# First forward stage of a fast Fourier transform on sums and differences of mirrored rows, as 24x24 matrices on 32x32 tiles

## The chip, the cores and the metric

The kernel runs on one core of a Trainium2 chip. The metric is the device time of one execution in microseconds (us). The engines named below are TensorE (PE in the profile, its weight loads PEld), VectorE (DVE), ScalarE (ACT), GpSimd (POOL) and SyncE (SP), whose queue issues most of the transfers. One slice of the work, a "slot", is explained below.

## The reference

A filter in the frequency domain over the sequence of each batch, then two dense layers with a GELU between them:

```python
batch, seq, dim = (8, 3008, 256)
X = np.fft.rfft(x, axis=1)
F = (filt_r + 1j * filt_i)[None, :, :]
y = np.fft.irfft(X * F, n=x.shape[1], axis=1)
...
h = x @ w_in                      # 24064 x 256 times 256 x 2048
g = 0.5 * h * (1.0 + erf(h * inv_sqrt2))
return (g @ w_out).astype(np.float32)
```

The input of the dense layers is the filtered sequence. Inputs and output are float32.

## The kernel before

The length 3008 is 47 x 64, and the transform is done in two factors each way. Row n of a batch is written as n = 64 m + w, with m from 0 to 46 and w from 0 to 63. Stage 1 (`s1`) is a transform over m, a multiplication with a table of 47 rows and 48 columns (24 frequencies, real and imaginary). Stage 2 (`s2`) is a transform over w with twiddles in the table, and is multiplied with the filter. Stages 3 and 4 (`s3`, `s4`) go back. Between stages 1 and 2, and between 3 and 4, the data pass through a buffer in DRAM (R1 and R2), which exchanges the axes: stores by SP, then loads (`r1`, `r2`). Stage 4 writes the bf16 ring `y_sb`, from which the dense layers read.

The dense layers go by tiles of 512 rows. A slot is one `mm1` (two matmuls of 512 columns for one of 16 blocks of hidden units, then GELU on ScalarE) and a quarter of the `mm2` of the tile before (four matmuls of 256 columns); every eight slots VectorE copies a result `ost` out of PSUM, and SP stores it. The slots of the first tile, 0 to 15, have no `mm2`. Batch 0 is transformed ahead of all slots by special routines (`c1` to `c4`). The stages of batches 1 to 7 are put between the slots by a list written by hand: `put(slot, function, batch, part)` files a step, and ahead of each slot its steps are issued. Each engine has one queue and works it off in that order, so a step on VectorE stands behind all VectorE steps filed before it.

Stage 1 of a batch is four calls `s1(b, c)`, at `s1 + int(c * n1)`: for batch 1 from slot 0 in steps of 4, for the others from `hi - 94` in steps of 3.5, where `hi` is the first slot that reads the batch. `r1` follows at slot 15 or `hi - 80`, the second stage at slot 25 or `hi - 69`. A call takes 16 of the 64 values of w:

- x lies in SBUF with m on partitions 0 to 46 for w below 32, and on 64 to 110 for the rest. `load_x` (L83) brings it from GpSimd's queue, which also turns float32 into bf16; eight loads per batch. In the second stage of the batch before, `load_next` files them one by one behind a `gate`, a copy of one element that makes GpSimd wait for the second stage's product.
- Eight matmuls (L300) of 47x64 by 512 columns run on four 64x64 tiles of TensorE into four PSUM banks, three of tag `f` (three in all) and one of tag `h` (three, else used by `mm1`).
- VectorE empties the four banks into `a_sb` (L275), and SP stores it to R1 in four transfers (L309) of 48 partitions.

The table `T1s` for this is made by `table_1_tiles` on GpSimd from the table of batch 0. GpSimd's queue at the start is: loads of x for batch 0, loads of the filters in three groups, `w_in`, copies of the filter to the other half of the partitions (`dup_filters`, L97), `T1s`, x of batch 1, `w_out`.

Of the kernel before, what the change touches and what calls it, by code (L numbers as in the profile page):

```python
# [9 lines left out]
AF = mybir.ActivationFunctionType  # L10
ALU = mybir.AluOpType
FP32 = mybir.dt.float32
BF16 = mybir.dt.bfloat16
I32 = mybir.dt.int32
PI = math.pi


NA, NB = 47, 64
K1 = 24
HB = 32  # L20
RND = 12582912.0
# [8 lines left out]
class _Mix:  # L30
    def __init__(self, ctx, tc, x, filt_r, filt_i, w_in, w_out, out):
        self.tc, self.nc = tc, tc.nc
        self.x, self.filt_r, self.filt_i = x, filt_r, filt_i
        self.w_in, self.w_out, self.out = w_in, w_out, out
        self.B, self.S, self.D = x.shape
        self.DFF = w_in.shape[1]
        assert self.S == NA * NB and self.D == 256 and self.DFF == 2048
        pool = lambda name, bufs, **kw: ctx.enter_context(tc.tile_pool(name=name, bufs=bufs, **kw))
        P = bass.MemoryType.PSUM
        self.const = pool("const", 1)  # L40
        self.px = pool("px", 2)
        self.pa = pool("pa", 3)
        self.pb = pool("pb", 4)
        self.pp = pool("pp", 4)
        self.pv = pool("pv", 3)
        self.pd = pool("pd", 4)
        self.pool = pool
        self.po = pool("po", 3)
        self.py = pool("py", 1)
        self.pg = pool("pg", 2)  # L50
        self.small = pool("small", 1)
        self.dram = pool("dram", 2, space=bass.MemoryType.DRAM)
        c = self.const
        self.T1 = c.tile([2 * NA, 96], BF16, name="T1")
        self.T2 = c.tile([128, K1, 2, NB], BF16, name="T2")
        self.T3 = c.tile([128, K1, 2, NB], BF16, name="T3")
        self.T4 = c.tile([96, NA, 2], BF16, name="T4")
        self.T4c = c.tile([96, NA, 2], BF16, name="T4c")
        self.F = c.tile([128, 2, K1, 256], BF16, name="F")
        self.w_in_sb = c.tile([128, 2, self.DFF], BF16, name="w_in_sb")  # L60
        self.w_out_sb = c.tile([128, 16, self.D], BF16, name="w_out_sb")
        self.ps, self.st = {}, {}
        self.flip = 0
# [11 lines left out]
    def load_x(self, b, lo=0, n=32, hs=(0, 1)):  # L75
        nc = self.nc
        if lo == 0 and 0 in hs:
            self.st[b, "x"] = self.px.tile([128 if b else 2 * NA, HB, 256], BF16, tag="x", name="x_sb")
        xt, o = self.st[b, "x"], 64 if b else NA
        xv = self.x[b].rearrange("(n1 h w) d -> h n1 w d", h=2, w=HB)  # L80
        for w in range(lo, lo + n, 8):
            for h in hs:
                nc.gpsimd.dma_start(out=xt[h * o:h * o + NA, w:w + 8, :], in_=xv[h][:, w:w + 8, :])  # L83

    def load_filters(self, k0, k):

# [14 lines left out]
        g = self.po.tile([1, 1], BF16, tag="gate", name="gate")  # L101
        self.nc.gpsimd.tensor_copy(out=g, in_=t)  # L102

    def load_next(self, b, p, c, h):

        self.gate(self.st[b, "p", p][0:1, 0:1])
        self.load_x(b + 1, 8 * c, 8, (h,))

    def load_w_in(self):
        wi = self.w_in.rearrange("(dc p) j -> p dc j", p=128)  # L110
# [14 lines left out]
    def table_1(self, g):  # L125

        nc, ts = self.nc, self.nc.vector.tensor_scalar
        col = lambda name: g.tile([128, 1], FP32, name=name)
        off = g.tile([128, 2, K1], FP32, name="off")
        nc.vector.memset(off[:, 0, :], 0.25)  # L130
        nc.vector.memset(off[:, 1, :], 0.5)
        h, n1, hs, hc = col("h"), col("n1"), col("hs"), col("hc")
# [144 lines left out]
            self.nc.vector.tensor_scalar(out=out, in0=in_, scalar1=scale, scalar2=None, op0=ALU.mult)  # L277


    def table_1_tiles(self, g):  # L280

        v = self.nc.gpsimd
        self.T1s = g.tile([128, 64], BF16, name="T1s")
        v.memset(self.T1s, 0.0)
        for r in (0, 64):
            v.tensor_copy(out=self.T1s[r:r + NA, 0:48], in_=self.T1[0:NA, 0:48])

    def s1(self, b, c):

        nc = self.nc  # L290
        if c == 0:
            self.st[b, "R1"] = self.dram.tile([NB, 48, 256], BF16, tag="R1", name="R1")
        a = self.pa.tile([128, 2, 4, 256], BF16, tag="a", name="a_sb")
        x = self.st[b, "x"]
        ps = [[self.bank("ps_s1", "h" if i == h == 0 else "f") for h in range(2)] for i in range(2)]
        for i in range(2):
            for r in range(2):
                for h in range(2):
                    w = 8 * c + 4 * r + 2 * i
                    nc.tensor.matmul(ps[i][h][64 * r:64 * r + 64, :], lhsT=self.T1s[64 * h:64 * h + NA],  # L300
                                     rhs=x[64 * h:64 * h + NA, w:w + 2, :], start=True, stop=True)
        for i in range(2):
            for h in range(2):
                self._evac(a[:, h, 2 * i:2 * i + 2, :].rearrange("p a b -> p (a b)"), ps[i][h], False)
        o = self.st[b, "R1"].rearrange("n q c -> q n c")
        for r in range(2):
            for h in range(2):
                w = HB * h + 8 * c + 4 * r
                nc.sync.dma_start(out=o[:, w:w + 4, :], in_=a[64 * r:64 * r + 48, h])  # L309

    def r1(self, b, c):
        bt = self.pb.tile([128, 6, 256], BF16, tag="b", name="b_sb")
# [219 lines left out]
def kernel(  # L532
# [40 lines left out]
    m.vt = m.pg.tile([128, 2, 97, 32], BF16, tag="g", name="vt_sb")  # L573
    for k, n in ((0, 4), (4, 8), (12, 12)):
        m.load_filters(k, n)
    m.load_w_in()

    nc.gpsimd.memset(m.vt[:, :, 96, :], 0.0)
# [35 lines left out]
    for q in range(1, 7):  # L614
        if q < 6:
            m.c2(2 * q)
            if q + 2 < 6:
                m.c1t(q + 2, (act,))
            if q != 3:
                m.warm_up(2)  # L620
            m.c2(2 * q + 1)
        if q < 6:
            m.c3(2 * q - 2)
            if q == 3:
                m.table_3(2)
                m.table_3_copy(2, True)
            else:
                m.warm_up(1)
        else:
            m.c3(10, 1)  # L630
            m.warm_up(1)
            m.c3(11, 1)
    m.warm_up(2)
    m.T1p = g.tile([2 * NA, 2, K1, 2], BF16, name="T1p")
    nc.gpsimd.tensor_copy(out=m.T1p, in_=m.T1.rearrange("p (h r k) -> p h k r", h=2, r=2))
    m.table_1_tiles(g)
    m.load_x(1)
    m.load_w_out(0)
    m.load_w_out(8)
    m.weights_4(g)  # L640
# [14 lines left out]
    def put(slot, f, *a):  # L655
        at.setdefault(slot, []).append((f, a))
# [4 lines left out]
    for b in range(1, B):  # L661
        hi = first(b)
        if b == 1:
            s1, n1, r1, s2, n2, r2, s4, n4 = 0, 4, 15, 25, 2.8, 61, 68, 0.72
        else:
            s1, n1, r1, s2, n2, r2, s4, n4 = hi - 94, 3.5, hi - 80, hi - 69, 3.5, hi - 24, hi - 17, 1
        for u in range(16):
            put(s4 + int(u * n4), m.s4, b, u // 2, u % 2)
        for c in range(4):
            put(s1 + int(c * n1), m.s1, b, c)  # L670
            put(r1, m.r1, b, c)
            put(r2, m.r2, b, c)
        for p in range(12):
            put(s2 + int(n2 * p), m.s2, b, p)
            put(s2 + int(n2 * p) + 4, m.s3, b, p)
        if b + 1 < B:
            for i in range(8):
                put(s2 + int(n2 * (i + 2)), m.load_next, b, i + 2, i // 2, i % 2)

    put(20, m.table_4, m.T4, m.T1p, m.wt, "f", "act")  # L680
    for s in range((NT + 1) * 16):
# [38 lines left out]
```

## Time and profile before

| what | us |
|---|---|
| time, median of 3 runs | 772.94 (771.6 to 773.65) |
| profiled execution: its span | 771.8 |
| TensorE busy | 763.0 (99%) |
| VectorE busy | 399.0 (52%) |
| ScalarE busy | 567.8 (74%) |
| GpSimd busy | 63.7 (8%) |
| matmuls of stage 1 (L300), 224, mean of one | 0.389 |
| evictions of stage 1 (L275 into `a_sb`), 112, mean of one | 0.683 |
| loads of x on GpSimd (L83), 64, mean of one | 0.516 |
| stores to R1 (L309), 112, median from issue to landing | 2.1 |
| loads from R1 (L315), 28, median from issue to landing | 4.2 |

In a busy column, rows that overlap on a pipelined engine count their own length; the ends of matmuls are modelled, so start-to-start distances say more than the mean of one. A timeline line gives start, length, engine, line of the code, operation, tiles (out<-in), shape, how many were merged, and in brackets how long the engine was idle before and for whom. A group line ends with busy us, the mean of one in ns, and the idle time before it. In a line by windows there follow, for each engine in the order PE, PEld, DVE, ACT, POOL, the busy us and in brackets the count, then the granted clock (1.00 is full), the busy share of the transfer engines and GB/s.

### The profile page before, as it was taken

What the parts mean: (1) busy time and instruction counts of PE and PEld (TensorE: products, weight loads), DVE (VectorE), ACT (ScalarE), POOL (GpSimd) and SP (SyncE); (2) the same over time, 40 slices, a digit from 0 to 9 for tenths busy, and PEclk for the clock granted to TensorE, in tenths of its full rate; (3) what the DMA queues carried; (4) which work ended last, traced back from release to release, by engine and by line L of the source; (5) the groups of instructions that cost most, each with busy time, mean ns of one, the idle gap of its engine ahead of it and who ended that gap; (6) DMA issues with size and microseconds to landing.
All of it is one profiled execution on the core that took longest, in us unless ns stands there. A gap on an engine that the chain in (4) does not pass through costs nothing.

```text
span 771.8 us, 15047 instructions
## 1 busy us (share of the span) xinstructions
PE 763.0 (99%) x6057; PEld 527.2 (68%) x6057; DVE 399.0 (52%) x735; ACT 567.8 (74%) x978; POOL 63.7 (8%) x157
## 2 busy tenths in 40 slices
PE   8999999999999999999999999999999999999998
PEld 4757675676776766667677767666776776766666
DVE  8966755464545645457463664637646366411011
ACT  7879855897568975699656996579865798666663
POOL 8701100010000200011000110001100000000000
PEclk9999999999999999999999999999999999999999
DMA  9795645466153661636516465355553422410111
GB/s 151 130 191 130 146 113 125 130 128 150 54 147 102 136 162 41 191 77 124 142 54 181 85 133 123 81 152 97 122 137 82 138 83 69 123 42 28 42 42 55
DMA packets 87270, 85.66 MB, mean 111 GB/s; under 512 B 6688, under 2 KB 77472, under 8 KB 87200
## 3 DMA queue, kind: packets, MB, share of 16 engines
q1 hardware_dynamic: 78816, 68.70, 31.6%
q0 software_dynamic: 8384, 16.00, 14.7%
q8 instruction: 47, 0.77, 0.4%
q14 instruction: 23, 0.19, 0.1%
HBM read 54.00 MB, written 46.66 MB: 130 GB/s over the span
## 4 chain that ended last, share of the span: by engine, by line
PE 97%; DMA 1%; DVE 1%; POOL 0%; issue 0%; SPq 0%; DVEq 0%; POOLq 0%
PE ps_o L513 42%; PE ps_h L486 42%; PE ps_s L373 2%; PE ps_s L348 2%; PE ps_s L323 2%; PE ps_s L300 2%; DMA x_sb<-in_x_dram 1%; PE ps_c L434 1%; PE ps_c3t L449 0%; PE ps_c L412 0%; DMA d_sb<-R 0%; PE ps_warm L267 0%; POOL x_sb L83 0%; PE ps_c L463 0%; DVE T3i L260 0%; PE ps_c1t L399 0%
## 5 line engine op out<-in xcount | busy, mean ns | idle before, releaser
L489 ACT ACTIVATE g_sb<-ps_h 128x512 bf16<-128x512 f32 x752 | 437.9, 597 | 182.7 <-PE ps_h L486 172.0
L513 PE MATMUL ps_o<-w_out_sb,g_sb 128*128 128x256 bf16 x2992 | 447.7, 273 | 0.0
L486 PE MATMUL ps_h<-y_sb,w_in_sb 128*128 128x512 bf16 (+3 forms) x1600 | 445.9, 366 | 0.3 <-DVE a_sb L275 0.3
L513 PEld LDWEIGHTS <-g_sb 128*128 128x128 bf16 x2992 | 283.8, 98 | 134.3 <-issue 9.9
L486 PEld LDWEIGHTS <-w_in_sb 128*128 128x128 bf16 x1600 | 154.8, 98 | 23.7 <-issue 1.3
L519 DVE COPY ost<-ps_o 128x512 f32<-128x512 f32 x93 | 63.9, 687 | 143.7 <-PE ps_o L513 143.6
L331 DVE TENSOR_TENSOR p<-ps_s,F 128x512 bf16<-128x512 f32 x84 | 58.1, 692 | 105.2 <-ACT p L330 89.1
L277 DVE TENSOR_SCALAR y_sb<-ps_s 128x376 bf16<-128x376 f32 x112 | 61.0, 548 | 80.7 <-PE ps_s L373 80.7
L275 DVE CAST a_sb<-ps_s 128x512 bf16<-128x512 f32 x112 | 69.5, 683 | 27.5 <-PE ps_s L300 26.5
L275 DVE CAST v_sb<-ps_s 128x512 bf16<-128x512 f32 x84 | 57.4, 685 | 2.9 <-PE ps_s L348 2.9
L329 ACT ACTIVATE p<-ps_s 64x512 bf16<-64x512 f32 x84 | 49.8, 593 | 2.1
L330 ACT CAST p<-ps_s 64x512 bf16<-64x512 f32 x84 | 48.5, 577 | 1.0
L373 PEld LDWEIGHTS <-d_sb 96*128 96x128 bf16 x448 | 30.8, 97 | 25.6 <-DMA d_sb<-R 0.6
L102 POOL COPY gate<-p 1x1 bf16<-1x1 bf16 x48 | 8.5, 176 | 469.0 <-DVE p L333 469.0
L333 DVE TENSOR_TENSOR p<-p 128x512 bf16<-128x512 bf16 x84 | 35.7, 425 | 2.9
L373 PE MATMUL ps_s<-T,d_sb 96*128 96x94 bf16 x448 | 36.3, 204 | 0.1
L332 DVE TENSOR_TENSOR p<-p,F 128x512 bf16<-128x512 bf16 x84 | 34.9, 416 | 0.0
L83 POOL DMA_DIRECT2D x_sb<-in_x_dram x64 | 32.9, 516 | 13.3 <-issue 12.2
L323 PE MATMUL ps_s<-b_sb,T 128*128 128x256 bf16 x168 | 32.1, 273 | 0.0
L348 PE MATMUL ps_s<-p,T 128*128 128x256 bf16 x168 | 32.1, 273 | 0.0
L348 PEld LDWEIGHTS <-T 128*128 128x128 bf16 x168 | 16.4, 98 | 19.8 <-DVE p L333 0.4
L323 PEld LDWEIGHTS <-T 128*128 128x128 bf16 x168 | 16.4, 98 | 13.4
(114 smaller groups left out, 196.1 us busy)
## 6 DMA issues: line engine op xcount, KB each, us to landing
out_dram<-ost SPq DMA_DIRECT2D x93, 256.0 KB, 2.5
x_sb<-in_x_dram POOLq DMA_DIRECT2D x64, 188.0 KB, 3.8
R<-a_sb SPq DMA_DIRECT2D x112, 96.0 KB, 2.1
b_sb<-R SPq DMA_DIRECT2D x28, 384.0 KB, 4.2
R<-v_sb SPq DMA_DIRECT2D x42, 256.0 KB, 3.5
d_sb<-R SPq DMA_DIRECT2D x56, 192.0 KB, 4.9
w_in_sb<-in_moe_w_in_dram POOLq DMA_DIRECT2D x2, 512.0 KB, 10.6
w_out_sb<-in_moe_w_out_dram POOLq DMA_DIRECT2D x2, 512.0 KB, 11.9
```

The lines of the kernel that those rows point to most:

```text
L275: self.nc.vector.tensor_copy(out=out, in_=in_)
L277: self.nc.vector.tensor_scalar(out=out, in0=in_, scalar1=scale, scalar2=None, op0=ALU.mult)
L323: nc.tensor.matmul(ps[:, 256 * i:256 * i + 256], lhsT=self.T2[:, k].rearrange("p a b -> p (a b)"), rhs=self.st[b, "b", k // 6][:, k % 6, : ...
L329: nc.scalar.activation(out=p2[0:64], in_=ps[64:128], func=AF.Copy, scale=-1.0)
L330: nc.scalar.copy(out=p2[64:128], in_=ps[0:64])
L331: nc.vector.tensor_tensor(out=p1, in0=ps, in1=f(0), op=ALU.mult)
L348: nc.tensor.matmul(ps[:, 256 * i:256 * i + 256], lhsT=self.T3[:, k].rearrange("p a b -> p (a b)"), rhs=w[:, 256 * i:256 * i + 256], start= ...
L373: nc.tensor.matmul(ps[:, 94 * i:94 * i + 94], lhsT=d[:, (grp % 2) * 4 + i, 128 * half:128 * half + 128], rhs=t4, start=True, stop=True)
L486: nc.tensor.matmul(ps[:, o:o + n], lhsT=self.w_in_sb[:, dc, jc * 128:jc * 128 + 128], rhs=self.ring[:, dc, off:off + n], start=(dc == 0), ...
L489: nc.scalar.activation(out=self.st["g", t][:, jc, :], in_=ps, func=AF.Gelu)
L513: nc.tensor.matmul(ps[:, tile_i % 2, :], lhsT=g[:, jc, tile_i * 128:tile_i * 128 + 128], rhs=self.w_out_sb[:, jc, :], start=(jc == 0), sto ...
L519: nc.vector.tensor_copy(out=ost, in_=ps)
```

## The change

With 47 rows, row m and row 47-m have the same cosine and opposite sines. So the real part of a stage 1 output needs only the sum of the two rows and the imaginary part only their difference, for m from 0 to 23 (row 0 stands with itself and is weighted by a half). The change makes the 47x48 table into two 24x24 ones.

- `load_pairs` replaces `load_x` for batches 1 to 7: an indirect gather brings, for four groups of 16 values of w, the rows m to partitions 32q + m, and a second one the rows 47-m to the same partitions. Two gathers per call of stage 1, each 128x1024. The indices are made by `row_indices` on GpSimd. The tile is 128x2x4x1024. `load_next` files both gathers of a part behind one gate, four times per batch.
- `fold`, filed two slots ahead of each `s1`, makes sum (into a new tile `xs`, one buffer) and difference (in place) on VectorE.
- `s1` issues 16 matmuls of 24x32 by 512 columns on sixteen 32x32 tiles: four groups of partitions times (two halves of the columns, sum and difference). VectorE empties four banks as before. SP stores to R1 in eight transfers of 24 partitions in place of four of 48.
- `angles_1_pairs`, `sines_1_pairs` and `table_1_pairs` make the new table on GpSimd and ScalarE. The first of them and `row_indices` are put between the groups of filter loads.
- In the list, batch 1's calls move from slots 0, 4, 8, 12 to 4, 7, 11, 14, and its `r1` from 15 to 17. The slots of the others are as before.

```diff
-    def load_next(self, b, p, c, h):
+    def load_next(self, b, p, g):
         self.gate(self.st[b, "p", p][0:1, 0:1])
-        self.load_x(b + 1, 8 * c, 8, (h,))
+        self.load_pairs(b + 1, g)
...
+    def load_pairs(self, b, c):
+        if c == 0:
+            self.st[b, "x"] = self.px.tile([128, 2, 4, 1024], BF16, tag="x", name="x_sb")
+        t = self.st[b, "x"]
+        rows = self.x.rearrange("b (n e) d -> (b n) (e d)", e=4)
+        for i in range(2):
+            self.nc.gpsimd.indirect_dma_start(
+                out=t[:, i, c], out_offset=None, in_=rows, element_offset=(b * self.S // 4 + c) * 1024,
+                in_offset=bass.IndirectOffsetOnAxis(ap=self.rows_at[i], axis=0))
...
+    def row_indices(self, g):
+        self.rows_at = [g.tile([128, 1], I32, name=n) for n in ("rows_d", "rows_m")]
+        for t, base, cm in zip(self.rows_at, (0, 16 * NA), (16, -16)):
+            for q in range(4):
+                self.nc.gpsimd.iota(t[32 * q:32 * q + 32], pattern=[[0, 1]], base=base + 4 * q, channel_multiplier=cm)
+        for q in range(4):
+            self.nc.gpsimd.iota(t[32 * q:32 * q + 1], pattern=[[0, 1]], base=4 * q, channel_multiplier=0)
+
+    def angles_1_pairs(self, g):
+        v = self.nc.gpsimd
+        m, self.half = (g.tile([128, 1], FP32, name=n) for n in ("m32", "half0"))
+        v.memset(self.half, 1.0)
+        for q in range(4):
+            v.iota(m[32 * q:32 * q + 32], pattern=[[0, 1]], base=0, channel_multiplier=1,
+                   allow_small_or_imprecise_dtypes=True)
+            v.memset(self.half[32 * q:32 * q + 1], 0.5)
+        v.tensor_scalar(out=m, in0=m, scalar1=1.0 / NA, scalar2=None, op0=ALU.mult)
...
+        v.tensor_scalar(out=w, in0=self.k48, scalar1=m, scalar2=None, op0=ALU.mult)
+        v.tensor_tensor(out=w, in0=w, in1=self.off, op=ALU.add)
+        v.tensor_scalar(out=r, in0=w, scalar1=RND, scalar2=-RND, op0=ALU.add, op1=ALU.add)
+        v.tensor_tensor(out=w, in0=w, in1=r, op=ALU.subtract)
+
+    def sines_1_pairs(self):
+        self.nc.scalar.activation(out=self.w1p, in_=self.w1p, func=AF.Sin, scale=2.0 * PI)
+
+    def table_1_pairs(self, g):
+        self.T1s = g.tile([128, 2, 32], BF16, name="T1s")
+        self.nc.gpsimd.memset(self.T1s, 0.0)
+        self.nc.gpsimd.tensor_scalar(out=self.T1s[:, :, 0:K1], in0=self.w1p, scalar1=self.half, scalar2=None,
+                                     op0=ALU.mult)
+
+    def fold(self, b, c):
+        x = self.st[b, "x"]
+        s = self.st[b, "fold", c] = self.pf.tile([128, 4, 256], BF16, tag="xs", name="xs")
+        d, m, s = x[:, 0, c], x[:, 1, c], s.rearrange("p a b -> p (a b)")
+        self.nc.vector.tensor_tensor(out=s, in0=d, in1=m, op=ALU.add)
+        self.nc.vector.tensor_tensor(out=d, in0=d, in1=m, op=ALU.subtract)
...
-        for i in range(2):
+        rows = (self.st.pop((b, "fold", c)), self.st[b, "x"][:, 0, c].rearrange("p (a b) -> p a b", a=4))
+        ps = [self.bank("ps_s1", "f" if g else "h") for g in range(4)]
+        for j in range(2):
             for r in range(2):
-                for h in range(2):
-                    w = 8 * c + 4 * r + 2 * i
-                    nc.tensor.matmul(ps[i][h][64 * r:64 * r + 64, :], lhsT=self.T1s[64 * h:64 * h + NA],
-                                     rhs=x[64 * h:64 * h + NA, w:w + 2, :], start=True, stop=True)
-        for i in range(2):
-            for h in range(2):
-                self._evac(a[:, h, 2 * i:2 * i + 2, :].rearrange("p a b -> p (a b)"), ps[i][h], False)
-        o = self.st[b, "R1"].rearrange("n q c -> q n c")
-        for r in range(2):
-            for h in range(2):
-                w = HB * h + 8 * c + 4 * r
-                nc.sync.dma_start(out=o[:, w:w + 4, :], in_=a[64 * r:64 * r + 48, h])
+                for g in range(4):
+                    o, w, k = 64 * j + 32 * r, 2 * j, slice(32 * g, 32 * g + K1)
+                    nc.tensor.matmul(ps[g][o:o + 32, :], lhsT=self.T1s[k, r, :],
+                                     rhs=rows[r][k, w:w + 2, :].rearrange("p a b -> p (a b)"), start=True, stop=True)
+        for g in range(4):
+            self._evac(a[:, g].rearrange("p a b -> p (a b)"), ps[g], False)
+        o = self.st[b, "R1"].rearrange("(g w) (r k) c -> r w k g c", g=4, r=2)
+        for j in range(2):
+            for r in range(2):
+                for i in range(2):
+                    p = 64 * j + 32 * r
+                    nc.sync.dma_start(out=o[r, 4 * c + 2 * j + i], in_=a[p:p + K1, :, i])
...
     for k, n in ((0, 4), (4, 8), (12, 12)):
         m.load_filters(k, n)
+        if k < 12:
+            (m.angles_1_pairs if k else m.row_indices)(g)
...
-            s1, n1, r1, s2, n2, r2, s4, n4 = 0, 4, 15, 25, 2.8, 61, 68, 0.72
+            s1, n1, r1, s2, n2, r2, s4, n4 = 4, 3.5, 17, 25, 2.8, 61, 68, 0.72
...
         for c in range(4):
+            put(s1 + int(c * n1) - 2, m.fold, b, c)
             put(s1 + int(c * n1), m.s1, b, c)
```

## The prediction

> **What bounds the kernel now.** I read the page first (busy shares, then the chain that ended last), then the timeline and the windows around one first stage. The first number of a group line is busy us, then the mean ns of one.
>
> ```profile
> PE 763.0 (99%) x6057; PEld 527.2 (68%) x6057; DVE 399.0 (52%) x735; ACT 567.8 (74%) x978; POOL 63.7 (8%) x157
> ...
> PE 97%; DMA 1%; DVE 1%; POOL 0%; issue 0%; SPq 0%; DVEq 0%; POOLq 0%
> ```
>
> TensorE is the bound: any wait that it gets is added to the span nearly in full, and any time taken off it is gained. VectorE is 52% busy on average, but the change acts in seven short stages, so what counts is VectorE there. One of them (batch 2), in order of time (start, us, engine, line):
>
> ```profile
> 114.02 0.69 DVE L519 COPY ost<-ps_o 128x512 f32<-128x512 f32 x1 [0.47 <-PE ps_o L513]
> 116.53 2.48 DVE L275 CAST a_sb<-ps_s 128x512 bf16<-128x512 f32 x4 [1.82 <-PE ps_s L300]
> 119.80 2.48 DVE L275 CAST a_sb<-ps_s 128x512 bf16<-128x512 f32 x4 [0.79 <-PE ps_s L300]
> 122.28 0.69 DVE L519 COPY ost<-ps_o 128x512 f32<-128x512 f32 x1
> 123.93 2.48 DVE L275 CAST a_sb<-ps_s 128x512 bf16<-128x512 f32 x4 [0.95 <-PE ps_s L300]
> 127.20 2.48 DVE L275 CAST a_sb<-ps_s 128x512 bf16<-128x512 f32 x4 [0.78 <-PE ps_s L300]
> ...
> 116.00:130.50 14.50, 14.50 (x116) 8.48 (x116) 10.63 (x17) 8.14 (x14) 0.00 (x0) 1.00 0.48 117
> ```
>
> In the window line VectorE is busy 10.63 of 14.5 us (the fourth figure): of a period of 3.3 us only 0.8 is free, once per call. The matmuls of the stage, and what stands after them:
>
> ```profile
> 116.08 0.63 PE L300 MATMUL ps_s<-x_sb,T1s 47*64 47x512 bf16 x8
> 116.63 0.28 PE L513 MATMUL ps_o<-w_out_sb,g_sb 128*128 128x256 bf16 x1
> ...
> L333 DVE TENSOR_TENSOR p<-p 128x512 bf16<-128x512 bf16 x84 | 35.7, 425 | 2.9
> L332 DVE TENSOR_TENSOR p<-p,F 128x512 bf16<-128x512 bf16 x84 | 34.9, 416 | 0.0
> ...
> 118.44 5.43 SPq L309 DMA_DIRECT2D R<-a_sb  x8
> 125.84 5.73 SPq L309 DMA_DIRECT2D R<-a_sb  x8
> 133.70 1.77 SPq L315 DMA_DIRECT2D b_sb<-R  x4
> ```
>
> The first calls stand at 116.08 and 126.81 in the chain: 10.73 us for ten slots and three calls. A slot (one `mm1` and one quarter of `mm2`) takes 0.87 us, so a call costs TensorE (10.73 - 8.7)/3 = 0.68 us.
>
> **What the Trainium skill says.** "TensorE: Matmul & The Clock Gate", Part 3, gives a span of one matmul plus about 4 ns for each further tile; the trace agrees for four tiles, whose eight matmuls start within 0.3 us. "TensorEngine Tiling (Array Packing)", PSUM Bottleneck, warns that tiling speeds TensorE but not the emptying of PSUM; here emptying takes 2.48 us of each call already. "VectorE: DVE Perf Modes", the perf-mode tier table, has a bf16 add of two SBUF tensors at half a cycle per element (1224 ns for 2048); the 416 to 425 ns above for 512 agree. No page prices an indirect gather.
>
> **The change, part by part.**
>
> *Matmuls.* 8 on four 64x64 tiles (two passes of 512 columns) become 16 on sixteen 32x32 tiles (one pass). A pass is 0.213 us (mm1: four of 512 and 0.87 per slot with four of 256, so 0.216); eight more starts at the skill's 4 ns are 0.04. Cost 0.68 - 0.213 + 0.04 = 0.51, gain 0.17 us per call, 28 calls: 4.8 us. Bounds: 6 us (starts free) and -8 us (tiles of one row group serialise: two passes more than now, +0.43 - 0.15 per call). I take 4.8.
>
> *Folds.* Two additions of 128x1024 per call. By the 425 ns for 512, of which 256/0.96 = 267 are elements, one takes 0.69 us; the second waits for the first (in the changed kernel's instruction order it waits on DVE itself), so 0.69 + 0.04 + 0.69 = 1.42 us. The average hides it (28 x 1.42 = 40 us of busy time on an engine half idle), the stage doesn't. In the changed kernel's instruction order each pair on VectorE stands behind the four evictions of the call before, though it is put two slots ahead of its own call, because calls are only 3 or 4 slots apart. So a cycle arises: matmuls start, first eviction 0.55 us later (0.45 now, where two banks are ready after the first pass; now all four end together), four evictions 0.60 apart, so the fold starts at 0.55 + 2.4 = 2.95, ends at 4.37, and the next matmuls start at 4.43. TensorE would be there after 2.61 + 0.51 = 3.12 us (3 slots) or 3.99 (4 slots). TensorE runs its queue in order: behind the waiting LDWEIGHTS stand all following `mm1` and `mm2`, and GELU behind those. Three intervals of 4.43 and 0.1 for the `ost` copy that the third must let pass: 13.4 us against 10.73, +2.65; the last call gives back 0.17; the first fold, behind the `ost` copy of 114.02, ends at 116.05 and costs 0.05. Batches 2 to 7: 6 x 2.55 = 15.3 us. Bounds: intervals of 4.33 (eviction after 0.45) give 13, of 4.7 give 20.
>
> *Stores.* 16 issues per batch become 32, of half the size. An issue takes 0.44 to 0.49 us in a row (1.77 for 4), so 8 take 3.8 us after each eviction; that fits into 4.43, and only the last eight count. In time from the first matmul of the batch: last call 13.4, evicted 16.45, stored 20.3, `ost` store 20.7; the load `r1` waits for landing (now 2.6 us from the start of the last issue), so issue at 22.4, landing 4.3 later: 26.7. The second stage stands at 140.34 - 116.08 = 24.26 now and 26.8 then. The cover of 2.3 us (138.0 against 140.34) is used up; with landings of 3.4 to 5.1 I take 0.4 per batch, 2.4 us in all; bounds 0 and 9. The slots of `s1` and `r1` of batches 2 to 7 are unchanged. The `ost` stores behind on SP have three buffers, one per 8 slots: nothing.
>
> *Batch 1.* Its slots hold only `mm1` (0.46 us), so nothing covers VectorE. Now the four calls run from 39.73, and slot 16 begins at 50.4. Then: slots 0 to 3 from 40.2, first call 42.15, fourth 42.15 + 3 x 4.43 = 55.45, slot 16 at 56.9: +6.5 us, of which TensorE gives nothing back. Evicted at 58.5, stored at 62.4, `r1` issued at 64.4, landed 68.7; the second stage (slot 25) is due at 56.9 + 7.86 = 64.8 and now starts at 58.26. It starts at 68.7: +10.5 us in all. Bounds: 6.5 (loads hidden) and 13.
>
> *The head.* POOL gets 12 iotas after the first filter loads (0.1 us each; they fall into 1.6 us that POOL waits[...] before the second loads: free) and 14 small operations before the third loads (0.1 to 0.3 us, 2.3 in all). Filter copies then begin at 19.4 instead of 17.2; `c2` needs them from 20.5 on, and the later ones have 0.9 to 1.5 us of slack. I take 0.5; bounds 0 and 2. One sine of ScalarE is 0.3 us, beside other work: nothing, at most 0.3.
>
> *Loads of x.* 8 gathers of 256 KB instead of 8 loads of 188 KB per batch. For batches 2 to 7 they are due some 33 us after issue: nothing. For batch 1 they follow at POOL 32; the first fold needs a pair by 40.1, the others one pair per 4.4 us. Half as many gates (4 instead of 8 a batch) stand ahead of them, and they bring 2 MB instead of 1.5 per batch onto transfer engines that the windows show 0.5 to 0.7 busy in those stages: nothing. At 0.5 us (the load row) to 2 us per issue and 3.8 to 5 us to land they are in time; at 4 us they would be late (below).
>
> **Sum.** 0.5 + 10.5 + 15.3 + 2.4 = 28.7 us; the matmul gain is inside the intervals. On the profiled execution, span 771.8, that is 800.5; its span lies 1.1 below the median of the runs (772.94), so 801.6.
>
> **Rivals.**
>
> *Same mechanism, likeliest:* 801.6, own range 790 to 815. For it: VectorE's evictions already fill 2.48 of 3.3 us.
>
> *Faster:* the fold doesn't reach the path. This needs, by 3.03 + fold against 3.12 and 3.99 us, a fold pair of at most 0.08 us to wait nowhere; at 0.40 the two waits of a batch eat its gain of 4 x 0.17. That is the point from which it decides: a fold ahead of the evictions, or one four times as cheap. Then 28 x 0.17 is kept, and 768 results. Against it: the instruction order and the 416 ns rows. It would need an operation that I have misread.
>
> *Slower by gathers or by serial tiles:* at 4 us per gather issue the last pair of batch 1 lands near 67 instead of 54, +13 us: 815. If tiles of one row group serialise, each of 21 intervals grows by about 0.65 and calls by 0.3: 817. For: neither is in the trace; against: eight tiles' starts lie together now, and a gather is one queue entry like a load.
>
> *No visible change:* the waits shrink to just the gain; only the cheap-fold bound allows it.
>
> **How the numbers follow.** Cadence 0.80, gathers or tiles 0.10, faster 0.07, unchanged 0.03. Predicted is 801.6. The range takes the bounds of the first case (low 788: head 0, batch 1 6.5, batches 13, less 5 for anything mis-sized) and reaches to the second: 788 to 815. Less or more than 0.3% (2.3 us) is what a measurement here can tell from none: faster 0.07, same 0.03, slower 0.90.
>
> **What would show it.** Starts of the first stage's matmuls 4.4 us apart, with VectorE without a gap between evictions and folds and TensorE idle before L348 for L333/L334's operand; 16 matmuls within 0.5 us; fold rows of 0.69 us; idle time of TensorE before batch 1's second stage put down to the load of `b_sb`; a busy share of TensorE near 95%. Wrong it would be if fold rows are below 0.3 us, if matmuls are 3.1 us apart, or if the span moves by less than 15 us.

## The result, and the profile after

The changed kernel takes 798.62 us, the median of four runs (797.55 to 799.87). The kernel before takes 773.24 us beside it (four runs). The ratio is 1.0331, with a 95% interval of 1.0314 to 1.0348. The profiled execution has a span of 798.1 us against 771.8, so 26.3 us are to be accounted for.

From the page of the changed kernel: the busy line, the chain that ended last, and one row of the costliest groups (first stage, real half).

```profile
PE 768.9 (96%) x6281; PEld 529.3 (66%) x6281; DVE 432.5 (54%) x791; ACT 568.7 (71%) x979; POOL 89.5 (11%) x158
...
PE 82%; DVE 8%; DMA 3%; issue 2%; POOL 2%; SPq 1%; ACT 1%; DVEq 0%; POOLq 0%
...
L348 PE MATMUL ps_s<-xs,T1s 24*32 24x512 bf16 x224 | 19.6, 387 | 9.4 <-DVE xs L333 9.4
```

TensorE was 99% busy and 97% of the chain. Now it is 96% and 82%; VectorE has taken 8% of the chain, though its own busy share rose only from 52% to 54%. That pair of numbers is the mark of a short stage with its own limit. The stage of batch 2, from the timeline of the changed kernel (TensorE first, then VectorE; start, length, engine, line):

```profile
129.34 0.39 PE L348 MATMUL ps_s<-xs,T1s 24*32 24x512 bf16 x4
...
129.38 0.40 PE L348 MATMUL ps_s<-x_sb,T1s 24*32 24x512 bf16 x4
129.71 0.61 PE L561 MATMUL ps_o<-w_out_sb,g_sb 128*128 128x256 bf16 x4
...
133.00 0.39 PE L348 MATMUL ps_s<-xs,T1s 24*32 24x512 bf16 x4 [0.51 <-DVE xs L333]
133.73 0.40 PE L348 MATMUL ps_s<-x_sb,T1s 24*32 24x512 bf16 x4 [0.33 <-DVE x_sb L334]
...
129.87 2.48 DVE L287 CAST a_sb<-ps_s 128x512 bf16<-128x512 f32 x4 [0.57 <-PE ps_s L348]
132.27 0.68 DVE L333 TENSOR_TENSOR xs<-x_sb 128x1024 bf16<-128x1024 bf16 x1
132.98 0.69 DVE L334 TENSOR_TENSOR x_sb<-x_sb 128x1024 bf16<-128x1024 bf16 x1
134.21 2.48 DVE L287 CAST a_sb<-ps_s 128x512 bf16<-128x512 f32 x4 [0.54 <-PE ps_s L348]
```

The sixteen matmuls of the first call start within 0.05 us, and the next `mm2` matmul stands 0.37 us behind the first of them (0.55 before: 116.08 to 116.63). So the tiles do on TensorE what they should. The second call waits for both folds, and the folds stand behind the four evictions of the call before. The single buffer of `xs` isn't what holds them: each sum begins as the last eviction ends, with no wait for TensorE to have read the sum before it. The evictions are 4.34 us apart, where they were 3.27 and 4.13 apart.

Now batch 1, from the timeline of the changed kernel: the stores of its first stage, the loads behind them, and the first matmul of its second stage.

```profile
47.15 17.95 SPq L357 DMA_DIRECT2D R<-a_sb  x32
66.48 1.77 SPq L363 DMA_DIRECT2D b_sb<-R  x4
69.74 0.61 PE L371 MATMUL ps_s<-b_sb,T 128*128 128x256 bf16 x2 [3.29 <-DMA b_sb<-R]
```

Two windows of the changed kernel (span, then busy us of TensorE, weight loads, VectorE, ScalarE and GpSimd; then the granted clock, the share of the transfer engines, GB/s). The first is the stage of batch 2, the second follows the wait of 3.29 us:

```profile
129.20:143.00 13.80, 12.13 (x127) 6.66 (x127) 12.05 (x21) 6.61 (x12) 0.00 (x0) 1.00 0.43 100
69.70:73.20 3.50, 3.46 (x14) 2.04 (x15) 1.45 (x3) 1.77 (x3) 0.00 (x0) 0.53 0.98 339
```

In the first, VectorE works 12.05 of 13.8 us and TensorE has 1.7 us of gaps. In the second TensorE is busy throughout, at half its clock. The Trainium skill ("TensorE: Matmul & The Clock Gate", Part 1, on the clock gate) says that the clock is halved after an idle window of about 3.4 us; the wait and the stretch that follows have that size here.

The 26.3 us lie in two places. The first call of batch 2 starts at 129.34 instead of 116.08, 13.26 later: that is the head and batch 1. From there to the end it is 668.8 us instead of 655.7: 13.1 for batches 2 to 7, 2.2 for each (96.2 us from one batch's first call to the next, 94.0 before). The 13.26 are 2.0 in the head (the last eviction of batch 0 ends at 42.13 instead of 40.13), 9.5 more up to batch 1's second stage (69.74 instead of 58.26), and the rest, about 1.7, in the stretch at half clock.

### The profile page after: what moved, and what is told of

The parts are those of the page before. It is cut to its first block, busy times and chain, and to the rows that moved or that the text cites. A ratio compares the mean times of both kernels' runs of the same rounds, so it can differ in the third digit from the quotient of the medians.

```text
span 798.1 us, 15648 instructions
## 1 busy us (share of the span) xinstructions
PE 768.9 (96%) x6281; PEld 529.3 (66%) x6281; DVE 432.5 (54%) x791; ACT 568.7 (71%) x979; POOL 89.5 (11%) x158
## 4 chain that ended last, share of the span: by engine, by line
PE 82%; DVE 8%; DMA 3%; issue 2%; POOL 2%; SPq 1%; ACT 1%; DVEq 0%; POOLq 0%
PE ps_o L561 37%; PE ps_h L534 36%; DVE a_sb L287 5%; PE ps_s L421 2%; PE ps_s L371 2%; PE ps_s L396 2%; DVE xs L333 1%; DMA R<-a_sb 1%; SPq L357 1%; PE ps_s L348 1%; DVE x_sb L334 1%; DMA x_sb<-in_x_dram 1%; ACT y_sb L285 1%; POOL F L104 1%; DVE ost L567 1%
## 5 line engine op out<-in xcount | busy, mean ns | idle before, releaser
L114 POOL COPY gate<-p 1x1 bf16<-1x1 bf16 x24 | 4.3, 181 | 462.9 <-DVE p L381 462.9
L396 PEld LDWEIGHTS <-T 128*128 128x128 bf16 x168 | 16.4, 98 | 19.8 <-DVE p L381 0.4
L348 PE MATMUL ps_s<-xs,T1s 24*32 24x512 bf16 x224 | 19.6, 387 | 9.4 <-DVE xs L333 9.4
L93 POOL DMA_INDIRECT x_sb<-in_x_dram,rows_d x28 | 27.1, 967 | 12.4 <-issue 9.0
```

The lines of the kernel that those rows point to most:

```text
L396: nc.tensor.matmul(ps[:, 256 * i:256 * i + 256], lhsT=self.T3[:, k].rearrange("p a b -> p (a b)"), rhs=w[:, 256 * i:256 * i + 256], start= ...
```

## The experiments

Three groups of four kernels ran, each group on one chip with the kernel before beside it (772.64, 772.5 and 772.75 us). A cause is read best from the traces' milestones, so they stand together here; "last store" is the start of the last store to R1 of batch 1, and the rightmost column is the span less the column before it.

| kernel | time, us | ratio (95%) | first call, batch 1 | last store | second stage, batch 1 | first call, batch 2 | from there to the end |
|---|---|---|---|---|---|---|---|
| before | 773.24 | 1 | 39.7 | 52.2 | 58.3 | 116.1 | 655.7 |
| changed | 798.62 | 1.0331 (1.0314-1.0348) | 44.1 | 64.7 | 69.7 | 129.3 | 668.8 |
| e1, no folds | 792.25 | 1.0248 (1.0218-1.0278) | 51.6 | 68.9 | 74.1 | 136.1 | 653.6 |
| e2, folds ahead | 791.2 | 1.0226 (1.0189-1.0263) | 53.4 | 72.6 | 77.8 | 136.8 | 653.8 |
| e3, table copied | 804.87 | 1.0414 (1.0397-1.0431) | 51.3 | 70.3 | 75.6 | 135.0 | 669.1 |
| e4, stores on two queues | 806.53 | 1.0441 (1.0424-1.0459) | 53.3 | 71.3 | 77.3 | 135.3 | 668.9 |
| e5, changed again | 799.32 | 1.0351 (1.0334-1.0367) | 44.7 | 64.6 | 69.6 | 127.6 | 668.8 |
| e6, plain loads | 797.58 | 1.0331 (1.0313-1.0349) | 43.6 | 62.8 | 68.0 | 125.9 | 668.8 |
| e7, wait filled | 800.72 | 1.0356 (1.0337-1.0375) | 44.8 | 64.4 | 71.7 | 130.6 | 669.3 |
| e8, batches 2 to 7 alone, ahead | 769.19 | 0.9956 (0.9941-0.9970) | 39.2 | 53.1 | 59.2 | 117.3 | 651.6 |
| e9, changed, third | 799.93 | 1.0346 (1.0315-1.0378) | 44.9 | 65.6 | 70.8 | 130.3 | 668.8 |
| e10, no folds again | 784.92 | 1.0163 (1.0145-1.0182) | 45.2 | 64.7 | 69.8 | 129.1 | 653.8 |
| e11, folds ahead again | 785.85 | 1.0167 (1.0149-1.0184) | 44.6 | 64.6 | 69.6 | 130.3 | 654.7 |
| e12, table copied again | 800.62 | 1.0358 (1.0338-1.0378) | 41.5 | 63.2 | 68.5 | 130.2 | 669.1 |

### The first group, and a stall of its own

Theory: the calls' intervals set by the folds make the loss, in batch 1 by way of the stores and the load of `b_sb`; the small operations on GpSimd make the head's 2 us. Rivals: the stores' own landing, the gathers, or the tiles. Four kernels, each with one part changed.

*e1, no folds.* The calls multiply the gathered rows as they are.

```diff
-            put(s1 + int(c * n1) - 2, m.fold, b, c)
...
-        rows = (self.st.pop((b, "fold", c)), self.st[b, "x"][:, 0, c].rearrange("p (a b) -> p a b", a=4))
+        rows = [self.st[b, "x"][:, i, c].rearrange("p (a b) -> p a b", a=4) for i in range(2)]
```

> The two additions per call are left out; the matmuls take the gathered rows as they are, so the sums and differences are not computed. Everything else (gathers, 32x32 tiles, 8 stores per call, new table) stays. Theory (VectorE's queue: evictions plus folds set the interval between calls): in batches 2 to 7 the calls stand 3.1 and 4.0 us apart instead of 4.35, TensorE waits nowhere for VectorE there, the 13 us of those batches go and the 0.17 to 0.18 us per call of the narrow tiles become visible, some 4 us more; batch 1 stays bound by its stores and the head stays late. Time 781.5, between 779 and 784. Rival (narrow tiles, gathers or the doubled stores are what costs): time stays above 792.

*e2, folds ahead.* In batches 2 to 7 the folds are filed before the end of the batch before them. There is no room for four buffers of sums, so the sum of part c goes into the place of the mirrored rows of part c-1, which have been used by then.

```diff
-            put(s1 + int(c * n1) - 2, m.fold, b, c)
+            put(s1 + int(c * n1) - 2 if b == 1 else first(b - 1) - 20 + 2 * c, m.fold, b, c)
...
-        s = self.st[b, "fold", c] = self.pf.tile([128, 4, 256], BF16, tag="xs", name="xs")
+        if c == 0:
+            s = self.pf.tile([128, 4, 256], BF16, tag="xs", name="xs")
+        else:
+            s = x[:, 1, c - 1].rearrange("p (a b) -> p a b", a=4)
+        self.st[b, "fold", c] = s
```

> The same folds, with the same result, but for batches 2 to 7 filed 20, 18, 16 and 14 slots ahead of the first slot of the batch before, so that they stand on VectorE ahead of the stage 4 evictions and not between the stage 1 evictions. Theory (place in the queue counts, not load): as without folds in these batches, 781.5, between 779 and 784.5, with VectorE as busy as in the changed kernel (432 us). Rival (the 38 us of added VectorE work count wherever they stand): above 790.

*e3, table copied.* `T1s` is filled by four copies of rows 0 to 31 of `T1`, with row 0 of each halved, in place of `angles_1_pairs` and `sines_1_pairs`.

```diff
-            (m.angles_1_pairs if k else m.row_indices)(g)
+            if k == 0:
+                m.row_indices(g)
...
-                m.sines_1_pairs()
...
+        for q in range(4):
+            self.nc.gpsimd.tensor_copy(out=self.T1s[32 * q:32 * q + 32, :, 0:K1],
+                                       in_=self.T1[0:32, 0:48].rearrange("p (r k) -> p r k", r=2))
...
```

> The new stage 1 table is copied on GpSimd from the table of batch 0 after the filter copies, in place of the 14 small operations between the filter loads and the sine on ScalarE. The 12 iotas of the row indices stay where they are. Theory (those 14 operations, 3.2 us between 14.5 and 17.7, are what holds the filter copies, for which VectorE waits 3.17 us once): that wait goes, batch 1 starts 1.9 us earlier: 796.7, between 795.8 and 798. Rival (the iotas or the transfers of the filters are what is late): no change, 798.6.

*e4, stores on two queues.* Half of batch 1's stores to R1 go to GpSimd's queue.

```diff
-                    nc.sync.dma_start(out=o[r, 4 * c + 2 * j + i], in_=a[p:p + K1, :, i])
+                    (nc.gpsimd if b == 1 and r else nc.sync).dma_start(out=o[r, 4 * c + 2 * j + i], in_=a[p:p + K1, :, i])
```

> Half of batch 1's stores to R1 (those of the differences, 16 of 32) are issued by GpSimd in place of SP. Theory (SP's issues, 24 of them still to come when the last eviction of batch 1 is near, make the second stage wait): the load b_sb starts some 2 us earlier, TensorE's wait for it shrinks from 3.3 to about 1.3 us and is too short for the clock to fall (0.53 for 3.5 us after it), which gives 1.6 us more: 795, between 794 and 796.5. Rival (the transfers beside the gathers and w_out are slow, whoever issues): within 1 us of 798.6.

All four missed in total, e1 and e2 by 10 us, and two of them came out slower than the changed kernel. The milestones show where: the first call of batch 1 begins at 51 to 53 us, 7 to 9 later than in the changed kernel. A window of e1 in the tail of batch 0 (columns as above):

```profile
35.00:40.00 5.00, 3.20 (x52) 2.59 (x49) 2.06 (x3) 0.33 (x2) 3.78 (x5) 1.00 0.97 145
```

And from the timeline of e4, ScalarE, which stands still for 7.42 us while GpSimd issues gathers:

```profile
44.50 1.24 ACT L285 ACTIVATE y_sb<-ps_c 128x376 bf16<-128x376 f32 x3 [7.42 <-PE ps_c3t L497]
```

TensorE works 3.20 of 5 us there; in the changed kernel it works all 5.00. Yet e4 differs from the changed kernel only in stores that come after 50 us. So its stall can't be due to the edit, and the totals of this group can't be set against 798.62. What the group does show lies behind the stall. From the first call of batch 2 on, e1 and e2 need 653.6 and 653.8 us where the changed kernel needs 668.8, and e3 and e4, which keep the folds in place, need 669.1 and 668.9. Batch 1 can be read too, from where it starts. From its first call to its second stage e1 takes 22.5 us and e2, which has the folds there, 24.3: without them the second stage comes 1.8 us sooner, not the 6.5 by which the prediction let them delay batch 1. In e4, with two queues for the stores, the loads of `b_sb` are issued 20.6 us after the first call, against 20.8 in e3 and 20.9 in e2; 2 us less were expected. With the folds still in place, dividing the issue brings next to nothing. In e1 the last eviction ends at 63.71, but SP goes on storing until 69.3. From its timeline, the last evictions and all the stores:

```profile
61.23 2.48 DVE L287 CAST a_sb<-ps_s 128x512 bf16<-128x512 f32 x4 [0.55 <-PE ps_s L348]
...
54.65 14.67 SPq L357 DMA_DIRECT2D R<-a_sb  x32
```

32 stores keep SP busy for 14.7 us, 0.46 each, even where VectorE is well ahead. In e1 none of them waits for an earlier store to land.

### The second group: the changed kernel again, loads, the wait, and a kernel that keeps only the gain

*e5, the changed kernel again.*

> The changed kernel itself once more, beside the others of this group. The four experiments before it all show 7 us lost between 36 and 45 us (TensorE busy under 3 of the 5 us from 35 to 40, ScalarE idle for over 7 us), which the profile of the changed kernel doesn't show. If that stall belongs to the chip on which they ran, it shows here too and the time is 806 (804 to 808). If it belongs to those programs, or comes by chance of where their instructions fall, the time is 798.6 (797 to 800) and TensorE is busy for all 5 us from 35 to 40.

799.32 us, with TensorE busy for 4.92 of the 5 us from 35 to 40: no stall. The first milestones agree with the first profile within 0.6 us. The first call of batch 2 is 1.7 sooner, though: that much differs between executions of the same program in batch 1.

*e6, plain loads.* The eight gathers of batch 1 become eight plain loads of as many bytes.

```diff
+            if b == 1:
+                k = b * self.S // 4 + 128 * (2 * c + i) % 512
+                self.nc.gpsimd.dma_start(out=t[:, i, c], in_=rows[k:k + 128])
+                continue
             self.nc.gpsimd.indirect_dma_start(
```

> Batch 1 takes its rows by eight plain loads of the same size in place of the eight indirect gathers (what is computed is left as it is; batch 1's data are other rows than the reference's, in other places). If it is the gathers that hold up the tail of batch 0 and the stores of batch 1 (13.9 us to land for w_out, stores ended at 65.1 us), the stall of 36 to 45 us is absent, the second stage of batch 1 starts 3 us or more sooner than in the changed kernel beside it, and the time is 3 us or more below it. If it is the bytes in flight, whatever fetches them, the time is that of the changed kernel within 1 us.

797.58 against 799.32, a difference of 1.7 us with ranges that overlap, between the two expectations. The milestones carry it: the last store leaves at 62.8 instead of 64.6, of which 1.1 us are there already at the first call (43.6 and 44.7), and SP waits 0.5 us for landing stores instead of 3.5. The gathers cost the head and batch 1 together something under 2 us. They aren't the cause of batch 1's 10.

*e7, the wait filled.* 14 matmuls on a constant stand ahead of the second stage of batch 1.

```diff
+        if b == 1:
+            put(s2, m.warm_up, 14, "f")
         for p in range(12):
             put(s2 + int(n2 * p), m.s2, b, p)
```

> 14 matmuls without a use are put into TensorE's wait for b_sb of batch 1 (nothing is left out). If the half clock after that wait (0.53 for 3.5 us from 69.7 us) comes from TensorE having stood idle, the clock stays at 1.0 there and the time falls by 1.6 us against the changed kernel beside it (1.0 to 2.5). If the drop has another cause, the clock falls in the same place and the time is the same within 0.5 us, or longer by what the filling delays.

800.72, the same within the ranges. In e5 the wait for `b_sb` was 0.9 us, not 3.29, and no half clock followed it. The filling took 3.0 us and so pushed the second stage from 69.6 to 71.7. There was nothing to win on this occasion, and the test by itself says nothing on the clock (the last section has what all traces together say). With e5 it does say that the stretch from 69.7 to 73.2 us in the first profile belonged to that execution: in e5 and e9 the half clock stands elsewhere.

*e8, batches 2 to 7 alone, with folds ahead.* Batch 1 keeps its former loads, table, tiles and slots. The other batches are as in e2, with the table copied as in e3, behind the loads of `w_out`.

```diff
-            put(s1 + int(c * n1) - 2, m.fold, b, c)
-            put(s1 + int(c * n1), m.s1, b, c)
+            if b > 1:
+                put(first(b - 1) - 20 + 2 * c, m.fold, b, c)
+            put(s1 + int(c * n1), m.s1 if b > 1 else m.s1_tiles, b, c)
...
-    m.table_1_pairs(g)
-    for i in range(4):
-        m.load_pairs(1, i)
+    m.table_1_tiles(g)
+    m.load_x(1)
     m.load_w_out(0)
     m.load_w_out(8)
     m.weights_4(g)
+    m.row_indices(g)
+    m.table_1_pairs(g)
```

> Batch 1 runs as in the kernel before (its loads, its 47x48 matrices on four tiles, its slots); batches 2 to 7 run the sixteen tiles, with the folds of a batch filed some 20 slots before the end of the batch before it, so that no call waits for its own; the small table is copied from the large one on GpSimd after the loads of w_out, and the row numbers are made there too. My theory (the loss is the interval between calls that the folds set, plus the head and batch 1; a call itself is 0.17 to 0.19 us cheaper on TensorE): 24 calls save 4.1 to 4.6 us, so 768.5 (767.3 to 769.7), with 93.25 us from one batch's first call to the next where the kernel before has 94.0. Rival (the calls' gain is eaten by VectorE's added 33 us or by stalls elsewhere): 772 or more.

769.19 us (768.11 to 772.22, eight runs), ratio 0.9956 (0.9941 to 0.9970): faster than both kernels, by 3.3 us on the kernel before. From its page the busy line, and from its timeline VectorE in the stage of batch 2:

```profile
PE 757.8 (99%) x6249; PEld 526.8 (69%) x6249; DVE 426.9 (56%) x783; ACT 568.2 (74%) x978; POOL 84.7 (11%) x154
```

```profile
117.83 2.48 DVE L287 CAST a_sb<-ps_s 128x512 bf16<-128x512 f32 x4 [1.89 <-PE ps_s L356]
120.91 2.49 DVE L287 CAST a_sb<-ps_s 128x512 bf16<-128x512 f32 x4 [0.59 <-PE ps_s L356]
123.31 0.68 DVE L606 COPY ost<-ps_o 128x512 f32<-128x512 f32 x1
124.86 2.48 DVE L287 CAST a_sb<-ps_s 128x512 bf16<-128x512 f32 x4 [0.86 <-PE ps_s L356]
```

VectorE does as many folds in batches 2 to 7 as in the changed kernel and is busier than before by 28 us; yet the evictions are 3.08 and 3.95 us apart, and VectorE waits for TensorE between them. A batch takes 93.28 us (from 117.3 to 583.7 in five), 0.72 less than 94.0, which is 0.18 per call. So the cost in the changed kernel was the place of the folds, not their amount. Of the expected 4.1 to 4.6 us, 1.2 went in batch 1, where the evictions of the fourth call waited 2.44 us for a store to land and with it for its buffer of `a_sb` (in the kernel before it was 1.03 us, and for TensorE).

### The third group: the first three again

*e9, the changed kernel a third time.*

> The changed kernel a third time, as the measure for the three beside it. If the stall of 36 to 45 us in the first four experiments belongs to their chip, then the changed kernel and the three beside it either all show it here (806 for this one) or none does (799); if it belongs to those programs, this one takes 799 and two or more of the three beside it lose 7 us between 36 and 45 us.

*e10, no folds (the edit of e1).*

> Once more without the folds (left out: the sums and differences; the matmuls read the gathered rows), beside the changed kernel. Batches 2 to 7 lose their 2.8 us each, 16.8 in all: about 782 where the changed kernel takes 799. If the calls' intervals in batch 1 (4.35 us) also set when its second stage starts, that goes too, and the time is 776 (774.5 to 778). If it is the landing of the gathers, of w_out and of the stores that sets it, nothing more is won: 781 to 783.

*e11, folds ahead (the edit of e2).*

> Once more with the folds of batches 2 to 7 filed ahead and batch 1 as in the changed kernel. From one batch's first call to the next 93.3 us where the changed kernel shows 96.2: 6 x 2.85 = 17.1 less, so 782 (780.5 to 783.5) where the changed kernel beside it takes 799. If the head and batch 1 bring a stall of their own in this program, as they did at first, 790.

*e12, table copied (the edit of e3).*

> Once more with the small table copied from the large one (no angles and no sines for it on GpSimd and ScalarE), beside the changed kernel. If the 3.2 us of small operations that go are what brought the head its 2.0 us (VectorE's wait of 3.17 us for the filter copies), the wait falls to 1.2 us and the time is 797 (796 to 798.3) where the changed kernel takes 799. If the head's delay is absorbed before the second stage of batch 1, 799.

None of the four has the stall. The same window in e10:

```profile
35.00:40.00 5.00, 4.92 (x86) 4.35 (x85) 3.62 (x7) 4.42 (x11) 3.82 (x4) 1.00 0.88 126
```

The three programs came out 7.3, 5.4 and 4.3 us faster than in the first group. The stall belonged to the chip of the first group, then, or to that occasion; the two aren't told apart. The kernel before, which doesn't gather in that stretch, took its usual time there. The changed kernel itself didn't run on that chip, and the cause stays open.

Without folds the time is 784.92, and with folds ahead 785.85; expected were 776 or 781 to 783, and 782, so both missed by 2 to 4 us. Both are 14 to 15 us shorter than the changed kernel from batch 2 on. But the head and batch 1 keep nearly all they had, and each has two or three waits for `b_sb` after batch 1 that the changed kernel has not (2.3 and 3.0 us in all). Most telling is e10, where the calls of batch 1 are free to follow one another. VectorE in its timeline:

```profile
45.70 2.48 DVE L287 CAST a_sb<-ps_s 128x512 bf16<-128x512 f32 x4 [2.49 <-PE ps_s L348]
48.73 2.48 DVE L287 CAST a_sb<-ps_s 128x512 bf16<-128x512 f32 x4 [0.55 <-PE ps_s L348]
51.75 2.48 DVE L287 CAST a_sb<-ps_s 128x512 bf16<-128x512 f32 x4 [0.55 <-PE ps_s L348]
57.35 2.48 DVE L287 CAST a_sb<-ps_s 128x512 bf16<-128x512 f32 x4 [3.11 <-DMA R<-a_sb]
```

And SP's stores to R1 in two pieces of the same timeline:

```profile
48.21 3.39 SPq L357 DMA_DIRECT2D R<-a_sb  x8
...
54.07 10.97 SPq L357 DMA_DIRECT2D R<-a_sb  x24
```

The first three calls are evicted 3.0 us apart, 1.3 us sooner each than with folds. SP stores the first call by 51.6 and then waits 2.4 us for one of these stores to land. The program is built so: in the trace SP's transfers signal eight semaphores in turn (111 to 118), and the ninth waits until the first has landed. With eight stores a call in place of four, that limit falls after one call and no longer after two. A step of the chain of e10 shows how long a landing takes beside the gathers and `w_out`:

```profile
49.42 6.43 DMA R<-a_sb
```

From 54.07 SP issues the other 24 stores without another long wait, 0.46 us each, until 65.0. The fourth call's evictions, held up by 3.11 us until the first call's stores had landed and freed its buffer, are done at 59.8 and don't matter. In the changed kernel VectorE is done at 60.5, and SP at 65.1. So batch 1 has a second limit of nearly the folds' length, SP's queue of 32 stores with the landing of the first eight in it. To take the folds of batch 1 away as well brings at most 0.9 us (784.92 against 785.85, with ranges that overlap). Half as many stores, a fourth buffer, or two queues without folds weren't tried.

With the table copied, the first call of batch 1 comes 3.4 us sooner than in e9 (41.5 against 44.9), and the time is the same (800.62 and 799.93). Two lines of e12, from the timeline and from the windows:

```profile
68.46 0.61 PE L375 MATMUL ps_s<-b_sb,T 128*128 128x256 bf16 x2 [4.19 <-DMA b_sb<-R]
```

```profile
66.80:74.20 7.40, 5.74 (x22) 3.28 (x23) 1.45 (x3) 3.42 (x6) 0.00 (x0) 0.54 0.63 229
```

The second stage starts 2.3 us sooner, after a longer wait for `b_sb`. Then TensorE runs at 0.54 of its clock until 74, which takes the 2.3 us back: batch 2 begins at 130.2 against 130.3. The small operations did delay the head, but in these two executions the time didn't hang on them. The expectation had 797 if it did, and 799 if the delay is absorbed on the way.

## Why the prediction was right

801.6 us was predicted and 798.62 came out. The point the forecast stood on, a fold pair that TensorE waits for at each call, is shown by experiment: batches 2 to 7 of e9 and e11 differ only in where the folds are filed and the sums are kept, and 14.1 us of the way from batch 2 to the end go with it. That the total is within 3 us owes something to luck: terms that were too small or missing (head 1.5, half clock 1.7) stand against terms that were too large (batch 1 1.0, folds 2.3, load of `b_sb` 2.4), and the reason given for the largest part of batch 1 was incomplete.

- **Matmuls: right.** A gain of 0.17 us per call was predicted, and 0.18 measured in e8. Sixteen starts within 0.05 us leave about 3 ns for each; the page of the Trainium skill that the prediction used for this ("TensorE: Matmul & The Clock Gate", Part 3) has 4. (The pass that was put at 0.213 us is 0.216 from start to start of 512 columns in the trace of the kernel before.) Tiles of one row group don't take turns, so the rival of serial tiles is out.
- **Folds: right in kind, 2.3 us too much in sum.** A fold takes 0.68 to 0.69 us, as worked out. The interval was to be 4.43 and is 4.34, since the first four matmuls start at 133.00, as soon as the sum is there, and the evictions follow the other twelve by 0.48 us instead of 0.55. Over six batches 13.1 us were lost, not 15.3. The price of the folds themselves is 2.9 us a batch: 96.2 less 93.3.
- **Load of `b_sb` in batches 2 to 7: 2.4 predicted, none found.** TensorE has no such wait there in the changed kernel. The waits appear once the folds are out of the way (2.3 us in e10, 3.0 in e11), and not in e8. Why e8 has none is open.
- **Batch 1: the size right, the reason in part wrong.** Predicted were 10.5 us up to the second stage; 9.5 came on top of the head's 2.0. The prediction laid 6.5 of it to three intervals of 4.43. Those intervals are there, and the last eviction ends at 60.5, which is the predicted 58.5 and the head's 2.0. But without the folds the second stage comes only 0.4 us sooner after the first call (24.6 us in e10, 25.0 in e11), and 1.8 in the first group. The step that failed is "that fits into 4.43, and only the last eight count", said of the eight stores of a call. Their issue does fit (3.4 to 3.8 us). But in batch 1 SP also waits for landings, 4.8 us in all in the changed kernel, and doesn't catch up: after the last eviction it needs 4.6 us there, and 4.0 and 4.6 in e5 and e9, where eight issues in a row take 3.4. In e10, where the evictions are sooner, the whole queue of 32 sets the end. So the folds and the stores are two limits of nearly equal length here, and the prediction had only the first.
- **Head: 0.5 predicted, 2.0 measured** to the last eviction of batch 0, the upper bound given. GpSimd's fourteen operations took 3.2 us instead of 2.3, and the filter copies began at 21.4 instead of 19.4. Yet e12 shows the 2 us aren't simply a term of the sum: taken away, they came back at half clock.
- **Gathers: near enough.** They take 0.95 to 1.08 us of GpSimd each and 0.3 us to the next, inside the bounds of 0.5 to 2. Plain loads in their place save 1.7 us up to batch 2, where nothing was charged; the ranges overlap.
- **Half clock: missing in the sum.** In the first profile 3.5 us at 0.53 cost about 1.65 us, by an estimate from these two figures (3.5 x (1 - 0.53)).

The rival on the faster side named its point: "a fold ahead of the evictions, or one four times as cheap. Then 28 x 0.17 is kept, and 768 results." e8 is that case for 24 of 28 calls, at 769.19 us.

## What to carry to other kernels

An engine that is half idle on average can still be full in the stage that is changed: count the period of that stage, and put added work where the stage is not. Work on data that arrived early, like these folds, cost no time when it was filed some 20 slots sooner (e8), and 2.9 us a batch in place. When transfers become more numerous and smaller, ask how many may be on their way at once. Where a stage has several limits of nearly equal length, as batch 1 had folds, store issue, landings and the clock, taking one away shows little, and the next in line has to be named.

## What the runs showed of the hardware that had not been expected

- TensorE's clock halved in one to four stretches of 3.4 us, or twice or three times that, in the first 80 us of each kernel with the new batch 1, at places that changed from run to run (49.1 and 69.6 us in the first profile of the changed kernel, 23.7 and 54.4 in the second, 24.3 and 58.4 in the third). The kernel before and e8 show none in that time. The traces also say when. Here are the pieces of 3.41 us just ahead of and in the two stretches of the first profile, then one of e9 that wasn't followed by a half clock, and the one after it:

```profile
45.69:49.10 3.41, 1.37 (x20) 0.35 (x19) 2.84 (x6) 1.07 (x3) 0.01 (x1) 1.00 1.17 179
49.10:52.51 3.41, 3.41 (x12) 0.98 (x11) 3.38 (x6) 2.00 (x4) 0.00 (x0) 0.50 1.39 201
66.17:69.58 3.41, 0.28 (x2) 0.00 (x0) 0.00 (x0) 0.64 (x2) 0.00 (x0) 1.00 0.57 173
69.58:72.99 3.41, 3.25 (x13) 1.94 (x14) 1.36 (x3) 1.77 (x3) 0.00 (x0) 0.50 0.98 339
...
68.67:72.08 3.41, 1.48 (x11) 0.97 (x11) 0.00 (x0) 1.43 (x3) 0.00 (x0) 1.00 0.95 320
72.08:75.49 3.41, 3.41 (x27) 2.48 (x26) 2.13 (x5) 3.32 (x7) 0.00 (x0) 1.00 0.56 206
```

  If each of the fourteen traces is divided into pieces of 3.41 us that fit its half-clock stretches, each of the 27 stretches in the first 80 us begins right after a piece in which TensorE was busy for 0 to 50% of the time. From 11 us on and at full clock, no piece above 50% was followed by one, every piece below 42% was, and between the two it went either way. So the place of a wait relative to these pieces counts, not only its length. The Trainium skill ("TensorE: Matmul & The Clock Gate", Part 1) speaks of an idle window; here pieces with 40% of work were enough. This is read from traces and wasn't tested by an edit.
- In the group on one chip of the three, all four kernels, which issue gathers between 33 and 43 us, lost some 7 us there, with ScalarE and VectorE served late by TensorE; three of these programs ran again on another chip with no such loss. The cause is open.
- A store to R1, which landed in a median of 3.3 us in batch 1 of the kernel before, took 6.4 us in e10 for one of the first call, beside the gathers and `w_out`. SP waited for such landings before it issued more, 3.7 us in all there, and 3.5 us in e5 against 0.5 with plain loads in e6.
